# Two numbers loaded first on ScalarE's queue, and a narrower bias table, in an attention and feed-forward kernel

## The chip, the cores and the metric

The kernel runs on one core of a Trainium2 chip. The metric is device time in microseconds (us) of one execution; several executions are timed and their median is given. Engines are named as the profile names them: PE is TensorE's matmul and PEld its weight load, DVE is VectorE, ACT is ScalarE, POOL is GpSimd and SP is SyncE, which here only issues transfers.

## The reference: what is computed

An attention over 2 batches, 8 heads, 768 positions and head width 64 comes first. A query sees a key if the key is one of the first `n_global` (8) positions, or lies 0 to `n_local`-1 (95) positions behind it. Its score gets a bias that falls with the distance. Both numbers are inputs (int64), so the kernel must read them at run time.

```python
rel = pos[:, None] - pos[None, :]
is_global = pos[None, :] < int(n_global)
is_local = (rel >= 0) & (rel < int(n_local))
keep = is_global | is_local
dist = np.where(is_global & ~is_local, float(n_local), np.abs(rel))
bias = -slopes[:, None, None] * dist[None, :, :]
scores = np.where(keep, scores + bias, -1e9)
a = softmax(scores)          # over keys
x = a @ v                    # then rows of 512
g = elu(x @ w_in)            # 1536 x 2048
x = g @ w_out                # 1536 x 512
h = max(x @ w1, x @ w2, x @ w3)   # 1536 x 768
return h @ w_out2
```

## The kernel before, in words

**Stages.** The attention is cut into 96 steps: a step is one pair of heads (`hp`) and one tile of 128 queries (`t`) of a group of 256 rows (`g`). A query tile needs only the 96 keys before it, the 8 global keys and its own 128 keys: 232 columns (`WIN = PREV + G + P`), or 128 for the first tile of a batch. Each step goes over the engines in turn. PE makes the scores (`scores_pe`, L217), DVE adds the bias and takes the minimum (`scores_dve`, L243), ACT takes the exponential and its row sum (`scores_act`, L264), DVE adds 1e-9 to the sum, inverts it and scales (`sums` L226, `recip` L255, `norm` L277), PE transposes (`turn_pe`, L287 and L293), ACT copies the transpose to SBUF (`turn_act`, L304), and PE multiplies with the values (`values_pe`, L316). The first 18 steps run in `windowed`, one after the other with steps interleaved, and between them the first feed-forward weights are unpacked from 64-bit words to 32 bits (`c_rebase`, `c_low`, `c_word`, `c_high`, `c_rest`). The others run inside the feed-forward loop (`Feed.run`), where PE's matmuls of 128x512 take most of the time.

**The order of the work is written by hand** (`tc.manual_schedule()`): each engine does its instructions in the order of the program text, and each queue of transfers is issued in that order too. Before the first step, `windowed` does the following.

- SP loads the queries and keys of the first pair of steps (`load_pair(0)`, L179), then the two numbers into `ni` (L51, in `numbers`), then the queries and keys of the next two pairs.
- POOL clears a tile `z`, and PE multiplies it by itself 8 times (`warm`, L587 and L593), a filler. Two more such fillers on `ident` follow each of the first two steps' scores.
- POOL writes position tables (`positions`, L79): `rel`, the distance of each of 360 columns, and the key number, in a scratch tile `sc`. The 360 columns are four pieces: 128 for a first tile (`P`), 96 keys before (`PREV`), 8 global keys (`G`), and 128 own keys. Only the first and the third piece can hold a global key; the other two get a key number of 2^20. Then POOL writes the scale of each head (`qsc`, L103) and `ident`, and scales the queries of each pair as it lands (`scale_queries`, L187).
- DVE sends negative distances to 1e30 (L144, L145), turns the loaded numbers from int64 to floats (L53, L56, L60), and makes the bias table from them (`bases`). It does four passes over all 360 columns: L155 marks columns with `rel >= nl`, L156 marks keys that aren't global, L157 joins the first mark with `rel`, and L158 takes the smaller of that and of `max(key mark, nl)`.

DVE's first score step (L243) reads the finished `rel`, so it stands behind all of this.

Of the kernel before, what the change touches and what calls it, by code (L numbers as in the profile page):

```python
# [13 lines left out]
I32 = mybir.dt.int32  # L14
# [3 lines left out]
ALU = mybir.AluOpType  # L18
# [5 lines left out]
P = 128  # L24
# [5 lines left out]
G = 8  # L30
PREV = 96
EXT = P + G
WIN = PREV + G + P
CH = WIN // 2
BIG = 1e30
# [9 lines left out]

def numbers(nc, pool, n_ap):

    ni = pool.tile([P, 4], I32, name="ni")  # L50
    nc.sync.dma_start(ni, n_ap.bitcast(I32).partition_broadcast(P))  # L51
    w = pool.tile([P, 4], F32, name="nw")
    nc.vector.tensor_copy(w, ni)  # L53
    w2 = w.rearrange("p (a b) -> p a b", b=2)
    hi = pool.tile([P, 2], F32, name="nhi")
    nc.vector.scalar_tensor_tensor(  # L56
        hi, w2[:, :, 0], 0.0, w2[:, :, 1], op0=ALU.is_lt, op1=ALU.add
    )
    nf = pool.tile([P, 2], F32, name="nf")
    nc.vector.scalar_tensor_tensor(  # L60
        nf, hi, 4294967296.0, w2[:, :, 0], op0=ALU.mult, op1=ALU.add
    )
    return nf[:, 0:1], nf[:, 1:2]


def covered(nc, pool, ng, nl, flag):

    f = pool.tile([P, 4], F32, name="nok")
    nc.vector.tensor_scalar(f[:, 0:1], ng, 0.0, None, op0=ALU.is_ge)
    nc.vector.tensor_scalar(f[:, 1:2], ng, float(G), None, op0=ALU.is_le)  # L70
    nc.vector.tensor_scalar(f[:, 2:3], nl, 1.0, None, op0=ALU.is_ge)
    nc.vector.tensor_scalar(f[:, 3:4], nl, float(PREV + 1), None, op0=ALU.is_le)
    ok = pool.tile([P, 1], F32, name="ok")
    nc.vector.tensor_reduce(ok, f, axis=AX.X, op=ALU.min)
    nc.vector.tensor_copy(flag, ok)


def iota(nc, t, num, step, base, cm):
    nc.gpsimd.iota(  # L79
        t, [[step, num]], base=base, channel_multiplier=cm,  # L80
        allow_small_or_imprecise_dtypes=True,
    )
# [15 lines left out]
def query_scales(nc, pool):  # L98

    qsc = pool.tile([P, HP], F32, name="qsc")  # L100
    for hp in range(HP):
        for u in range(2):
            nc.gpsimd.memset(  # L103
                qsc[u * D:u * D + D, hp:hp + 1], -(2.0 ** (2 * hp + u + 1)) * D ** -0.5
            )
    return qsc


class Windowed:
# [17 lines left out]
    def positions(self, scratch):  # L127

        nc, c = self.nc, self.const
        n = P + WIN  # L130
        rel = c.tile([P, n], F32, name="rel")
        key, neg = scratch[0][:, 0:n], scratch[1][:, 0:n]
        far = 1 << 20
        o = 0
        for num, step, base, cm, kstep, kbase in (
            (P, -1, 0, 1, 1, 0),
            (PREV, -1, PREV, 1, 0, far),
            (G, 0, far, 0, 1, 0),
            (P, -1, 0, 1, 0, far),
        ):  # L140
            iota(nc, rel[:, o:o + num], num, step, base, cm)
            iota(nc, key[:, o:o + num], num, kstep, kbase, 0)
            o += num
        nc.vector.tensor_scalar(neg, rel, 0.0, BIG, op0=ALU.is_lt, op1=ALU.mult)  # L144
        nc.vector.tensor_tensor(rel, rel, neg, op=ALU.max)  # L145
        self.qsc = query_scales(nc, c)
        self.ident = c.tile([P, P], F32, name="ident")
        make_identity(nc, self.ident)
        self.base, self.key, self.tmp = rel, key, neg

    def bases(self, ng, nl, a, b):


        nc, rel, key, t = self.nc, self.base[:, a:b], self.key[:, a:b], self.tmp[:, a:b]
        nc.vector.tensor_scalar(t, rel, nl, BIG, op0=ALU.is_ge, op1=ALU.mult)  # L155
        nc.vector.tensor_scalar(key, key, ng, BIG, op0=ALU.is_ge, op1=ALU.mult)  # L156
        nc.vector.tensor_tensor(t, t, rel, op=ALU.max)  # L157
        nc.vector.scalar_tensor_tensor(rel, key, nl, t, op0=ALU.max, op1=ALU.min)  # L158

    def geom(self, s):  # L160

# [608 lines left out]
def dense_attention(tc, ctx, io, xd):  # L770
# [4 lines left out]
    p2 = ctx.enter_context(tc.tile_pool(name="dp", bufs=2))  # L775
    ps = ctx.enter_context(tc.tile_pool(name="dps", bufs=1, space=PSUM))
    ng, nl = numbers(nc, c, io["nn"])
    qsc = query_scales(nc, c)
    ident = c.tile([P, P], F32, name="ident")
# [69 lines left out]
def windowed(tc, ctx, io, flag):  # L849
    nc = tc.nc  # L850
    f = Feed(tc, ctx, io)
    at = Windowed(tc, ctx, io, f.ps, f.xy, f.wt, f.act)
    with tc.manual_schedule():
        scratch = [f.cv.tile([P, 512], F32, tag="wr", name="sc") for _ in range(2)]
        at.load_pair(0, True)
        f.warm(WARM)
        at.positions(scratch)
        ng, nl = numbers(nc, at.const, io["nn"])
        for p in range(1, 3):
            at.load_pair(p, True)  # L860
        at.scale_queries(0)
        at.bases(ng, nl, 0, P + WIN)
        first = BLOCKS[0] // GRP * 8
        x = f.split_tiles()

        def convert():
            f.c_rebase(0)
            f.c_low(0)
            yield
            f.c_word(0, 0)  # L870
            yield
            f.c_word(0, 1)
            yield
            f.c_high(0)
            f.c_rebase(1)
            f.c_low(1)
            yield
            f.c_word(1, 0)
            yield
            f.c_rest(0)  # L880
            yield
            f.c_word(1, 1)
            yield
            f.c_high(1)
            f.c_rebase(2)
            f.c_low(2)
            yield
            f.c_rest(1)
            yield
            f.c_word(2, 0)  # L890
            yield
            f.c_word(2, 1)
            yield

        words = convert()
        h = f.ps.tile([P, 512], F32, tag="h", name="h")
        for k in range(first + 2):
            e = k % 2
            at.load_values(k, True)
            if e == 0:  # L900
                at.load_pair(k // 2 + 3, k < first)
                at.scale_queries(k // 2 + 1)
            if k <= first:
                at.scores_pe(k, (("S0", "S1"), ("y0", "y1"))[e], 1 + (k == first))
            if k >= first:
                f.product(h, f.w[0][:, 0], x, GRP, 0, (k - first) * 6, 6)
            at.values_pe(k - 3)
            at.turn_pe(k - 2, ("TX", "y2", "y3")[k % 3])
            if k < FILL[0]:
                f.fill(at.ident, FILL[1])  # L910
            at.scores_dve(k, True)
            at.values_high(k - 3, x)
            at.turn_act(k - 2, nc.scalar.copy)
            at.scores_act(k)
            at.sums(k - 1)
            at.recip(k - 1)
            at.norm(k - 1)
            at.values_low(k - 3, x)
            if k >= CONV:
                next(words, None)  # L920
            if k in WLOAD:
                f.w_load()
        at.values_pe(first - 1)
        at.turn_pe(first, "TX")
        at.values_high(first - 1, x)
        at.turn_act(first, nc.scalar.copy)
        at.sums(first + 1)
        at.values_low(first - 1, x)
        at.recip(first + 1)
        at.norm(first + 1)  # L930
        next(words, None)
        f.run(at, first + 2, x, h, lambda: covered(nc, at.const, ng, nl, flag))
# [105 lines left out]
```

## Time and profile before

| | before |
|---|---|
| median of 3 runs | 570.06 us (569.61 to 570.16) |
| profiled execution, its own time | 570.73 us |
| span of the profiled execution | 568.7 us |
| mean granted TensorE clock, share of 2.4 GHz | 0.991 |
| PE busy, share of the span | 547.9 us, 96% |
| DVE busy | 323.9 us, 57% |
| ACT busy | 267.9 us, 47% |
| POOL busy | 77.8 us, 14% |

The span runs from the first to the last instruction of one execution; 2.0 us of that execution's own time lie around it. Busy shares are means over stages with different limits: DVE is nearly full in the first 150 us and idle for much of the rest, and PE is the other way about in the first 50 us.

### The profile page before, as it was taken

What the parts mean: (1) busy time and instruction counts of PE and PEld (TensorE: products, weight loads), DVE (VectorE), ACT (ScalarE), POOL (GpSimd) and SP (SyncE); (2) the same over time, 40 slices, a digit from 0 to 9 for tenths busy, and PEclk for the clock granted to TensorE, in tenths of its full rate; (3) what the DMA queues carried; (4) which work ended last, traced back from release to release, by engine and by line L of the source; (5) the groups of instructions that cost most, each with busy time, mean ns of one, the idle gap of its engine ahead of it and who ended that gap; (6) DMA issues with size and microseconds to landing.
All of it is one profiled execution on the core that took longest, in us unless ns stands there. A gap on an engine that the chain in (4) does not pass through costs nothing. (4 is left out here: it accounts for less than half of the span.)

```text
span 568.7 us, 7611 instructions
## 1 busy us (share of the span) xinstructions
PE 547.9 (96%) x2772; PEld 434.2 (76%) x2772; DVE 323.9 (57%) x732; ACT 267.9 (47%) x574; POOL 77.8 (14%) x87
## 2 busy tenths in 40 slices
PE   8788999999999999999999999999999999999995
PEld 6457777777777777777888888888887888888884
DVE  7998999999755444343466656567754112312112
ACT  5877777777656455554555564524323101311011
POOL 4100222222210000000011221023320000000000
PEclk9979999999999999999999999999999999999998
DMA  8918444432211111010013323122302000010002
GB/s 295 379 45 328 172 156 159 168 133 65 77 39 43 42 41 42 20 55 2 0 38 111 94 92 112 37 75 80 118 24 76 0 1 1 15 60 1 0 1 80
DMA packets 16670, 46.62 MB, mean 82 GB/s; under 512 B 1776, under 2 KB 1776, under 8 KB 16624
## 3 DMA queue, kind: packets, MB, share of 16 engines
q1 hardware_dynamic: 15760, 44.47, 22.9%
q10 hardware_dynamic: 864, 1.57, 0.8%
q8 instruction: 24, 0.39, 0.3%
q14 instruction: 22, 0.18, 0.1%
HBM read 42.90 MB, written 3.15 MB: 81 GB/s over the span
## 5 line engine op out<-in xcount | busy, mean ns | idle before, releaser
L505 PE MATMUL h<-xh,w 128*128 128x512 f32 (+1 forms) x536 | 144.3, 391 | 0.6 <-ACT xh L485 0.6
L505 PEld LDWEIGHTS h<-xh,w 128*128 128x128 f32 x536 | 98.3, 188 | 23.7 <-issue 1.7
L536 PE MATMUL y<-gh,w 128*128 128x512 f32 x384 | 98.7, 399 | 0.0
L512 ACT CAST gh<-e 128x512 fp32r<-128x512 f32 x66 | 41.1, 622 | 101.8 <-DVE e L725 87.1
L725 DVE TENSOR_TENSOR e<-S,e 128x512 f32<-128x512 f32 x36 | 24.9, 692 | 103.6 <-PE S L505 100.5
L536 PEld LDWEIGHTS y<-gh,w 128*128 128x128 f32 x384 | 69.6, 188 | 18.1 <-issue 1.5
L505 PE MATMUL h<-xl,w 128*128 128x512 f32 (+1 forms) x268 | 82.0, 387 | 0.0
L505 PE MATMUL S<-xh,w 128*128 128x512 f32 x288 | 77.0, 389 | 0.0
L530 DVE SCALAR_TENSOR_TENSOR e<-e,h 128x512 f32<-128x512 f32 x48 | 33.0, 687 | 68.0 <-ACT e L526 68.0
L505 PEld LDWEIGHTS S<-xh,w 128*128 128x128 f32 x288 | 54.1, 188 | 11.2
L525 ACT ACTIVATE e<-h 128x512 f32<-128x512 f32 x48 | 28.4, 592 | 67.7 <-PE h L505 67.4
L462 POOL TENSOR_TENSOR w<-wr,w 128x512 fp32r<-128x512 f32 x24 | 35.3, 1473 | 166.0 <-ACT w L461 166.0
L505 PEld LDWEIGHTS h<-xl,w 128*128 128x128 f32 x268 | 50.0, 188 | 10.5 <-DVE xl L486 0.2
L517 DVE TENSOR_TENSOR gl<-e,gh 128x512 fp32r<-128x512 f32 x50 | 39.8, 796 | 31.8 <-ACT gh L512 31.6
L264 ACT ACTIVATE p<-p,m 128x232 f32<-128x232 f32 (+1 forms) x96 | 44.8, 468 | 25.4 <-DVE m L243 25.4
L544 PE MATMUL y<-gl,w 128*128 128x512 f32 x192 | 51.5, 390 | 0.0
L415 DVE SCALAR_TENSOR_TENSOR wr<-wr 128x1024 uint32<-128x1024 uint32 (+1 forms) x36 | 50.0, 1397 | 0.7
L505 PE MATMUL S<-xl,w 128*128 128x512 f32 x144 | 44.3, 389 | 0.0
L451 DVE SCALAR_TENSOR_TENSOR wr<-wr 128x512 uint32<-128x512 uint32 x48 | 43.0, 896 | 2.2
L544 PEld LDWEIGHTS y<-gl,w 128*128 128x128 f32 x192 | 36.0, 188 | 7.9 <-issue 0.3
L569 PE MATMUL y<-w,gh 128*128 128x512 f32 x144 | 37.3, 390 | 0.4 <-POOLq L942 0.4
L517 POOL TENSOR_TENSOR gl<-e,gh 128x512 fp32r<-128x512 f32 x16 | 21.0, 1311 | 104.9 <-ACT gh L512 104.9
(85 smaller groups left out, 600.2 us busy)
## 6 DMA issues: line engine op xcount, KB each, us to landing
wr<-wa SPq DMA_DIRECT2D x14, 1024.0 KB, 7.6
wr<-wb SPq DMA_DIRECT2D x24, 512.0 KB, 3.3
v<-v SPq DMA_DIRECT2D x24, 256.0 KB, 2.7
raw<-qk SPq DMA_DIRECT2D x16, 312.0 KB, 3.3
raw<-qk SPq DMA_DIRECT2D x8, 260.0 KB, 3.4
wr<-wa SPq DMA_DIRECT2D x4, 512.0 KB, 3.7
out<-ot ACTq DMA_DIRECT2D x6, 256.0 KB, 3.0
out<-ot SPq DMA_DIRECT2D x6, 256.0 KB, 2.5
```

Of the source, the lines that this page charges most:

```text
L264: self.nc.scalar.activation(p[:, o], p[:, o], AF.Exp, bias=m[:, u:u + 1], scale=-1.0, accum_out=m[:, 2 + u:3 + u],)
L415: self.nc.vector.scalar_tensor_tensor(r[..., 0], r[..., 1], v, r[..., 0], op0=op, op1=ALU.bitwise_or)
L451: self.nc.vector.scalar_tensor_tensor(t, a, c, t, op0=op, op1=ALU.bitwise_or)
L462: nc.gpsimd.tensor_tensor(w[:, j % 2, 1], v, w[:, j % 2, 0].bitcast(F32), op=ALU.subtract)
L505: nc.tensor.matmul(out[:, o:n], w[:, part % 2, c * P:c * P + P], (xl if part == 2 else xh)[:, c, o:n], start=c == 0 and part == 0, stop=c ...
L512: self.nc.scalar.copy(gh[:, 0:n], e[:, 0:n])
L517: (engine or self.nc.vector).tensor_tensor(gl[:, 0:n], e[:, 0:n], gh[:, 0:n].bitcast(F32), op=ALU.subtract)
L525: self.nc.scalar.activation(e, h, AF.Relu, scale=-1.0)
L530: self.nc.vector.scalar_tensor_tensor(e, e, -1.0, h, op0=ALU.add, op1=ALU.max)
L536: self.nc.tensor.matmul(y[e][:, 0:n], w[:, a, e * P:e * P + P], g[0][:, 0:n], start=fc == 0 and a == 0, stop=False,)
L544: self.nc.tensor.matmul(y[e][:, 0:n], w[:, 0, e * P:e * P + P], g[1][:, 0:n], start=False, stop=fc == NFC - 1,)
L569: nc.tensor.matmul(o[r], gh[:, r * P:r * P + P], w[:, a], start=j == 0 and a == 0, stop=False,)
```

## The change

The load of the two numbers leaves `numbers` and becomes `load_numbers`. In `windowed` it is the first thing issued, and it goes on ACT's queue in place of SP's. The other half of `numbers` (the conversion) now stands behind the loads of pairs 1 and 2 in the text. `positions` writes key numbers only for the two pieces that can hold a global key, which drops two iotas. `bases` does two passes over 360 columns (mark, then join into `rel`), and two passes (key mark, then minimum) over the 128 and over the 8 columns where a key can be global. Line numbers behind L50 move by up to 10: `norm` is L286 after the change, `scores_dve` L252.

```diff
-def numbers(nc, pool, n_ap):
-
+def load_numbers(nc, pool, n_ap):
     ni = pool.tile([P, 4], I32, name="ni")
-    nc.sync.dma_start(ni, n_ap.bitcast(I32).partition_broadcast(P))
+    nc.scalar.dma_start(ni, n_ap.bitcast(I32).partition_broadcast(P))
+    return ni
+
+
+def numbers(nc, pool, n_ap, ni=None):
+
+    ni = load_numbers(nc, pool, n_ap) if ni is None else ni
     w = pool.tile([P, 4], F32, name="nw")
...
-        for num, step, base, cm, kstep, kbase in (
-            (P, -1, 0, 1, 1, 0),
-            (PREV, -1, PREV, 1, 0, far),
-            (G, 0, far, 0, 1, 0),
-            (P, -1, 0, 1, 0, far),
+        for num, step, base, cm, keys in (
+            (P, -1, 0, 1, True),
+            (PREV, -1, PREV, 1, False),
+            (G, 0, far, 0, True),
+            (P, -1, 0, 1, False),
         ):
             iota(nc, rel[:, o:o + num], num, step, base, cm)
-            iota(nc, key[:, o:o + num], num, kstep, kbase, 0)
+            if keys:
+                iota(nc, key[:, o:o + num], num, 1, 0, 0)
             o += num
...
-    def bases(self, ng, nl, a, b):
-
-
-        nc, rel, key, t = self.nc, self.base[:, a:b], self.key[:, a:b], self.tmp[:, a:b]
-        nc.vector.tensor_scalar(t, rel, nl, BIG, op0=ALU.is_ge, op1=ALU.mult)
-        nc.vector.tensor_scalar(key, key, ng, BIG, op0=ALU.is_ge, op1=ALU.mult)
-        nc.vector.tensor_tensor(t, t, rel, op=ALU.max)
-        nc.vector.scalar_tensor_tensor(rel, key, nl, t, op0=ALU.max, op1=ALU.min)
+    def bases(self, ng, nl):
+
+
+        v, rel, key, t = self.nc.vector, self.base, self.key, self.tmp
+        v.tensor_scalar(t, rel, nl, BIG, op0=ALU.is_ge, op1=ALU.mult)
+        v.tensor_tensor(rel, t, rel, op=ALU.max)
+        for o in (slice(0, P), slice(P + PREV, P + PREV + G)):
+            v.tensor_scalar(key[:, o], key[:, o], ng, BIG, op0=ALU.is_ge, op1=ALU.mult)
+            v.scalar_tensor_tensor(
+                rel[:, o], key[:, o], nl, rel[:, o], op0=ALU.max, op1=ALU.min
+            )
...
+        ni = load_numbers(nc, at.const, io["nn"])
         at.load_pair(0, True)
         f.warm(WARM)
         at.positions(scratch)
-        ng, nl = numbers(nc, at.const, io["nn"])
         for p in range(1, 3):
             at.load_pair(p, True)
+        ng, nl = numbers(nc, at.const, io["nn"], ni)
         at.scale_queries(0)
-        at.bases(ng, nl, 0, P + WIN)
+        at.bases(ng, nl)
```

DVE's order at the start, before the change, from the end of the position tables to the first score step (`nf` holds the two numbers as floats, `sc` is scratch, `S_153` and `S_154` are the scores of the first step's two heads):

```order
L53 CAST nw<-ni 128x4
L56 SCALAR_TENSOR_TENSOR nhi<-nw 128x2
L60 SCALAR_TENSOR_TENSOR nf<-nhi,nw 128x2
L155 TENSOR_SCALAR sc<-rel,nf 128x360
L156 TENSOR_SCALAR sc<-sc,nf 128x360
L157 TENSOR_TENSOR sc<-sc,rel 128x360
L158 SCALAR_TENSOR_TENSOR rel<-sc,nf 128x360
L243 ISA p,m<-S_153,rel 128x128
```

The same place after the change:

```order
L58 CAST nw<-ni 128x4
L61 SCALAR_TENSOR_TENSOR nhi<-nw 128x2
L65 SCALAR_TENSOR_TENSOR nf<-nhi,nw 128x2
L161 TENSOR_SCALAR sc<-rel,nf 128x360
L162 TENSOR_TENSOR rel<-sc,rel 128x360
L164 TENSOR_SCALAR sc<-sc,nf 128x128
L165 SCALAR_TENSOR_TENSOR rel<-sc,nf,rel 128x128
L164 TENSOR_SCALAR sc<-sc,nf 128x8
L165 SCALAR_TENSOR_TENSOR rel<-sc,nf,rel 128x8
L252 ISA p,m<-S_153,rel 128x128
```

Two passes of 360 columns have become two of 128 and two of 8, and `sc`'s pass no longer stands between the mark and the join.

ACT's order at the start, after the change (before, the load of the exponential's table was its first row, and the numbers' transfer was the second on SP):

```order
L50 DMA ni<-nn 128x4
L273 ACT_TABLE_LOAD
L273 ACTIVATE p,m<-p,m 128x128 x2
L273 ACTIVATE p,m<-p,m 128x232 x2
L313 COPY p<-y_192 128x256
```

The transfer stands ahead of the table load on ACT, and no transfer stands ahead of it on that queue.

POOL's position tables, after the change (before, an iota on `sc` followed each of the four on `rel`):

```order
L84 IOTA rel 128x128
L84 IOTA sc 128x128
L84 IOTA rel 128x96
L84 IOTA rel 128x8
L84 IOTA sc 128x8
L84 IOTA rel 128x128
L108 MEMSET qsc 64x1 x8
```

The 96-wide and the second 128-wide iota on `sc` are gone; on the other engines no row has moved.

## Rows read from the trace of the kernel before

**Rows 1.** Busy time by stretch; columns: stretch, length, PE, PEld, DVE, ACT, POOL, PEclk, DMA.

```profile
20.00:25.00 5.00, 3.24 (x28) 2.03 (x28) 4.86 (x18) 3.93 (x15) 0.40 (x1) 1.00 1.04 396
28.00:29.70 1.70, 0.32 (x5) 0.00 (x1) 1.63 (x11) 1.70 (x4) 0.00 (x0) 0.99 0.11 43
29.70:36.40 6.70, 6.70 (x36) 4.23 (x38) 6.56 (x22) 4.31 (x15) 0.00 (x0) 0.50 0.26 88
45.00:47.00 2.00, 0.66 (x8) 0.42 (x9) 1.93 (x9) 1.57 (x6) 0.00 (x0) 1.00 1.01 412
50.00:57.00 7.00, 6.94 (x48) 5.54 (x49) 5.49 (x13) 6.39 (x13) 1.29 (x1) 1.00 0.87 318
200.00:300.00 100.00, 99.99 (x522) 79.38 (x521) 45.15 (x121) 50.42 (x110) 3.59 (x4) 1.00 0.10 31
```

**Rows 2.** Timeline, DVE's start; columns: start us, us, instruction, count, [idle before <-releaser].

```profile
2.49 0.53 DVE L145 TENSOR_TENSOR rel<-rel,sc 128x360 f32<-128x360 f32 x1
4.02 0.20 DVE L53 CAST nw<-ni 128x4 f32<-128x4 int32 x1 [0.99 <-DMA ni<-nn]
...
4.54 0.16 DVE L60 SCALAR_TENSOR_TENSOR nf<-nhi,nw 128x2 f32<-128x2 f32 x1
4.74 0.41 DVE L155 TENSOR_SCALAR sc<-rel,nf 128x360 f32<-128x360 f32 x1
5.06 0.40 DVE L156 TENSOR_SCALAR sc<-sc,nf 128x360 f32<-128x360 f32 x1
5.38 0.53 DVE L157 TENSOR_TENSOR sc<-sc,rel 128x360 f32<-128x360 f32 x1
5.94 0.69 DVE L158 SCALAR_TENSOR_TENSOR rel<-sc,nf 128x360 f32<-128x360 f32 x1
6.78 0.29 DVE L243 CUSTOM_DVE_ANT_0 p<-S,rel 128x128 f32<-128x128 f32 x1 [0.16 <-DVE rel L158]
...
7.53 0.40 DVE L243 CUSTOM_DVE_ANT_0 p<-y,rel 128x232 f32<-128x232 f32 x1
```

**Rows 3.** Timeline, SP's queue, its first two issues.

```profile
0.73 0.40 SPq L179 DMA_DIRECT2D raw<-qk  x1
1.18 0.42 SPq L51 DMA_DIRECT2D ni<-nn  x1
```

**Rows 4.** Line L51, the numbers' transfer, from issue to landing.

```profile
DMA to landing us min/median/max: 2.8/2.8/2.8
```

**Rows 5.** Line L747, six output stores on ACT's queue, from issue to landing.

```profile
DMA to landing us min/median/max: 2.0/3.0/4.4
```

**Rows 6.** Timeline, ACT's first instruction.

```profile
0.73 1.28 ACT L264 ACT_TABLE_LOAD   x1 [0.73 <-PEq L1028]
```

**Rows 7.** Timeline, POOL: the dropped iotas, the first scaling.

```profile
1.50 0.21 POOL L79 IOTA sc<- 128x96 f32 x1
...
2.02 0.24 POOL L79 IOTA sc<- 128x128 f32 x1
...
4.02 0.48 POOL L187 TENSOR_SCALAR raw<-raw,qsc 128x256 f32<-128x256 f32 x1
```

**Rows 8.** Timeline, DVE: narrow passes, and scaling pairs with and without POOL beside them.

```profile
8.43 0.72 DVE L277 TENSOR_SCALAR p<-p,m 128x128 f32<-128x128 f32 x2
...
11.67 0.48 DVE L277 TENSOR_SCALAR p<-p,m 128x128 f32<-128x128 f32 x2
12.07 0.28 DVE L332 TENSOR_TENSOR xl<-y,xh 128x128 fp32r<-128x128 f32 x1
...
13.21 0.59 DVE L277 TENSOR_SCALAR p<-p,m 128x232 f32<-128x232 f32 x2
...
26.42 0.82 DVE L277 TENSOR_SCALAR p<-p,m 128x232 f32<-128x232 f32 x2
```

**Rows 9.** Timeline, PEld and PE: the scores of the first two steps.

```profile
4.70 0.51 PEld L217 LDWEIGHTS S<-raw 64*128 64x128 f32 x4 [0.22 <-POOL raw L187]
...
6.22 0.66 PE L217 MATMUL y<-raw 64*128 64x232 f32 x4
```

## Prediction
> **What bounds the kernel now.** I read the table of busy time by stretch first, because the page's share for PE (96%) is a mean over stages with different limits. From 20 to 25 us DVE is busy 4.86 of 5.00 us while PE has 3.24; from 200 to 300 us PE is busy 99.99 of 100.00 [rows 1]. So the opening is DVE's, the body PE's. The chain of waits that ended last is PE from start to end and tells nothing of the opening, so I turned to DVE's timeline there. DVE stands idle 0.99 us until the two numbers land, converts them, makes the bias table from 4.74 us on, and starts its first score step at 6.78, released by that table [rows 2]. From 6.78 on DVE hardly stops. Everything the change touches lies ahead of 6.78, on the chain load, conversion, table, first score. What that chain gains should pass through a saturated DVE into a saturated PE and to the end, unless another engine or a transfer takes its place.
>
> **The load.** SP issues it second, at 1.18 us, behind the first pair's queries at 0.73 [rows 3], and it lands 2.8 us later [rows 4], just ahead of its reader at 4.02. Now ACT issues it as its first instruction; ACT, whose table load starts at 0.73 today [rows 6], is ready at the same time as SP. With the same 2.8 us the numbers come 1.18 - 0.73 = 0.45 us earlier, and the conversion starts at 3.57. Bounds come from the nearest transfers on ACT's queue, six output stores that took 2.0 to 4.4 us [rows 5]. At 2.0 us the reader would be held by the pass L145 instead, which ends at 2.49 + 0.53 = 3.02 us and moves 0.17 us with POOL's iotas (one dropped iota stands ahead of `rel`'s last): 2.89, a gain of 1.1. At 4.4 us the numbers land at 5.13, a loss of 1.15. I take 2.8, since that is this very transfer. The table load behind it on ACT starts about 0.4 us later and ends near 2.4 us; ACT's first exponential waits for the score step at 6.78, so this costs nothing.
>
> **The table.** Today it takes 6.78 - 4.74 = 2.04 us from its first pass to the score step [rows 2]. The new six passes, start to start: the mark of 360 columns, 0.41 and 0.04 of hand-over (from L60's end, 4.54 + 0.16 = 4.70, to 4.74), 0.45; the join, 0.53 long, with a successor that doesn't read its result and so may start 0.09 earlier, as L156 does behind L155 (0.32 against 0.41), 0.44; the key mark of 128 columns, 0.28 (the pair takes 0.48 and its second starts 0.20 later [rows 8]) and hand-over, 0.32; the minimum of 128 columns, priced as the 128-wide tensor pass of 0.28 less 0.09, 0.20; two passes of 8 columns at 0.20 each, as L60 to L155. The sum is 1.81, a gain of 0.23, say 0.25. Bounds: with every pass paying its whole length and hand-over it is 0.45 + 0.57 + 0.32 + 0.32 + 0.20 + 0.20 = 2.06, no gain; with the last three overlapped and no hand-over about 1.55, a gain of 0.5.
>
> A rule speaks against this edit. The Trainium skill, VectorE: DVE Perf Modes, section "The TRN2 errata — SBUF-src ops pay a fixed extra latency per instruction", puts a measured fixed term of about 150 cycles (0.156 us) on each instruction beside its columns; four passes would then cost 4 x 0.156 + 1080/960 = 1.75 us and six 6 x 0.156 + 744/960 = 1.71 (estimates, with plain scalar passes at two columns a cycle), a gain of 0.04. L145 agrees with the fixed term ((360 + 151)/960 = 0.53 us), but L156's start 0.32 us behind a pass of 0.41 shows that part of it overlaps.
>
> **POOL, SP and PE.** The two dropped iotas are each followed 0.17 to 0.18 us later by the next instruction, so POOL's first scaling, at 4.02 now [rows 7], comes 0.35 us earlier, at 3.67; the first pair lands at 0.73 + 2.8 = 3.53 and doesn't hold it. PE's first scores waited 0.22 us for that scaling [rows 9], so PE moves up by up to 0.22. SP's later issues move up by 0.45 us; no consumer in the opening waits on those loads except POOL, which has time. Nothing else is moved: the fallback path also loses and gains rows, but isn't run.
>
> **Sum.** 0.45 + 0.25 = 0.70 us: the first score step at about 6.08. PE caps it: the second step's scores end at 6.22 + 0.66 = 6.88, less 0.22 is 6.66, and DVE reads the last of them at 7.53 now, 6.83 then. So the cap is just clear; a faster landing would gain 0.87 at most. The cover for the shift afterwards is DVE's own load. Against the profiled execution's 570.73 us that makes 570.0; that execution stands 0.67 above the median of the runs, so I subtract from the median: 570.06 - 0.70 = **569.4 us**.
>
> **Rivals.**
> 1. *The gain halves or goes*: six passes pay in full (table gain 0), or ACT's queue lands at its stores' 3.0 us or later (load gain 0.25 or less). By the first alone 570.06 - 0.45 = 569.6; by both 569.8. For it: L157 to L158 takes 0.56, no overlap, where one reads the other. Against it: L155 to L156.
> 2. *Collisions with POOL vanish*: three of DVE's scaling pairs, the first at 8.43 and the last at 26.42, take 0.24 us more than the same pair elsewhere (0.72 against 0.48, 0.82 against 0.59 [rows 8]); each falls beside one of POOL's scalings, whose times follow the landings. DVE moves by 0.70 and the landings by 0.3 to 0.45, so some may part: 3 x 0.24 = 0.72 more, 568.6. Against it: others may meet instead.
> 3. *The clock drops in a costly place* (slower). PE's granted clock goes to 0.50 (1.2 GHz) from 29.7 to 36.4 us, behind a stretch in which PE was busy 0.32 of 1.70; it costs nothing, since DVE is full there (6.56 of 6.70). From 45 to 47 PE is as idle (0.66 of 2.00) and no drop follows. From 50 to 57 PE has 6.94 of 7.00 [rows 1]. If the shift let such a drop begin by 50, half of 6.7 us, 3.35, would be lost: 570.06 - 0.70 + 3.35 = 572.7. It decides from the moment the drop covers PE's full stretch. Against it: the runs before, within 0.55 us, show no sign of it.
> 4. *The load isn't first*: the table load holds it, issue at 0.73 + 1.28 = 2.01, landing at 4.81, 0.83 late, less 0.25: 570.6. Against it: the order of ACT's rows.
>
> **How the numbers follow.** Forecast 0.57, rival 1 0.18, rival 2 0.13, rival 3 0.07, rival 4 0.05. A measurement here can tell about 0.2%, 1.14 us: under 568.92 is faster, over 571.20 slower. Faster comes from rival 2 and a little of the forecast's upper end, 0.16; slower from rival 3 and the worst landing, 0.09; within, 0.75. The range takes in rivals 1, 2 and 4 and leaves out rival 3: 568.6 to 570.6.
>
> **What would show it.** The numbers' issue on ACT at 0.73 and a reader near 3.6; table passes spaced 0.45, 0.44, 0.32, 0.20, 0.20, 0.20; the first score near 6.1 in place of 6.78; the same lead, 0.6 to 0.8 us, at the first matmul of 512 columns near 51 us and at the end. I am wrong if the reader is no earlier than 4.0, if the lead is lost before 50 us, or if the granted clock is low in another stretch.

## The result, and the profile after

The change makes the kernel slower, by 0.7%. Over 20 runs each the median goes from 569.73 us to 575.05 us; the ratio of after to before is 1.0066 with a 95% interval of 1.0042 to 1.0089. The times lie in two groups, and the change moves runs from one to the other: before, 17 of 20 runs stand at 568.7 to 570.9 us and 3 at 575.3 to 575.7; after, one stands at 570.2 and 19 at 573.3 to 576.6. The median so jumps by a whole group; the means of the 20 times, 570.58 and 574.94, lie 4.4 us apart. The profiled execution after took 575.05 us with a span of 573.0 us and a mean granted clock of 0.978, against 568.7 us and 0.991 before.

**The loads.** The timelines of ACT's and SP's queues after the change, with the first issue of each:

```profile
0.74 0.41 ACTq L50 DMA_DIRECT2D ni<-nn  x1
```

```profile
0.73 1.35 SPq L188 DMA_DIRECT2D raw<-qk  x3
```

The numbers' issue moved as planned, from 1.18 [rows 3] to 0.74. Issue to landing of that load (its line's view) and of the first three loads of queries and keys:

```profile
DMA to landing us min/median/max: 4.3/4.3/4.3
```

```profile
DMA to landing us min/median/max: 4.1/4.4/4.6
```

The numbers now take 4.3 us in place of 2.8 [rows 4]. The first pair, the quickest of the three, takes 4.1 us in place of 2.8; before the change it had landed by about 3.5 us, ahead of its reader, POOL's first scaling, at 4.02 [rows 7].

**DVE's start after**, its timeline to the first score step:

```profile
2.33 0.53 DVE L151 TENSOR_TENSOR rel<-rel,sc 128x360 f32<-128x360 f32 x1
5.02 0.40 DVE L58 CAST nw<-ni 128x4 f32<-128x4 int32 x1 [2.15 <-DMA ni<-nn]
...
5.84 0.52 DVE L161 TENSOR_SCALAR sc<-rel,nf 128x360 f32<-128x360 f32 x1
6.40 0.54 DVE L162 TENSOR_TENSOR rel<-sc,rel 128x360 f32<-128x360 f32 x1
6.86 0.42 DVE L164 TENSOR_SCALAR sc<-sc,nf 128x128 f32<-128x128 f32 x1
7.32 0.35 DVE L165 SCALAR_TENSOR_TENSOR rel<-sc,nf,rel 128x128 f32<-128x128 f32 x1
7.59 0.23 DVE L164 TENSOR_SCALAR sc<-sc,nf 128x8 f32<-128x8 f32 x1
7.85 0.35 DVE L165 SCALAR_TENSOR_TENSOR rel<-sc,nf,rel 128x8 f32<-128x8 f32 x1
8.12 0.28 DVE L252 CUSTOM_DVE_ANT_0 p<-S,rel 128x128 f32<-128x128 f32 x1
```

The wait for the numbers grew from 0.99 to 2.15 us, the conversion starts at 5.02 instead of 4.02, and the table takes 8.12 - 5.84 = 2.28 us instead of 2.04 [rows 2]. The first score step is 1.34 us late.

**PE's start after**, its timeline, and POOL's first two scalings:

```profile
0.98 3.79 PE L602 MATMUL z<-z 128*128 128x128 f32 x16 [0.98 <-POOL z L596]
5.45 0.49 PE L226 MATMUL S<-raw 64*128 64x128 f32 x4 [0.68 <-POOL raw L196]
...
8.51 0.65 PE L226 MATMUL S<-raw 64*128 64x128 f32 x4 [0.70 <-POOL raw L196]
10.30 0.52 PE L296 MATMUL y<-ident,p 128*128 128x128 f32 x2 [1.14 <-DVE p L286]
...
20.05 1.15 PE L226 MATMUL y<-raw 64*128 64x232 f32 x4
```

```profile
4.91 0.48 POOL L196 TENSOR_SCALAR raw<-raw,qsc 128x256 f32<-128x256 f32 x1 [1.29 <-DMA raw<-qk]
5.69 0.48 POOL L196 TENSOR_SCALAR raw<-raw,qsc 128x256 f32<-128x256 f32 x1 [0.29 <-DMA raw<-qk]
```

The first scaling waits 1.29 us for the first pair, and PE, whose fillers are done, waits for that scaling (0.68 us), then 0.70 us until 8.51, and, before the first transpose, for the late scaling in `norm` on DVE (1.14 us). Such waits of PE are called holes below. The profile puts the second down to POOL, but the second pair's scaling had ended by 6.17. The third step's scores go into the tiles that DVE reads in its first score step, and here and in experiments 1, 2, 3, 7, 8 and 9 they start 0.38 to 0.40 us behind the start of that step (8.12 here). So the first hole comes with the late first pair and the second with the late numbers. Before, the first was 0.22 us of weight load [rows 9], the second wasn't there, and the third was nearly as long (1.08 us).

**What follows**, busy time by stretch after the change (columns as in [rows 1]):

```profile
10.00:15.00 5.00, 4.70 (x30) 2.83 (x30) 4.46 (x27) 3.36 (x14) 0.48 (x1) 0.70 1.03 401
15.00:20.00 5.00, 5.00 (x26) 2.91 (x26) 3.14 (x19) 3.21 (x12) 0.76 (x2) 0.50 1.04 394
20.00:25.00 5.00, 5.00 (x26) 2.81 (x26) 3.88 (x19) 3.51 (x12) 0.80 (x2) 0.50 0.48 173
25.00:30.00 5.00, 5.00 (x27) 2.78 (x28) 4.88 (x15) 3.78 (x14) 1.10 (x1) 0.59 0.75 239
...
200.00:300.00 100.00, 99.99 (x532) 79.18 (x533) 44.78 (x126) 50.42 (x113) 2.76 (x4) 1.00 0.10 32
```

The granted clock falls to 0.50 (1.2 GHz) near 12 us and stays there until about 29; the same four score matmuls take 1.15 us in place of 0.66 [rows 9]. And here DVE isn't full: from 20 to 25 us it has 3.88, where it had 4.86 [rows 1]. Its timeline there says on whom it waits:

```profile
18.47 0.29 DVE L252 CUSTOM_DVE_ANT_0 p<-S,rel 128x128 f32<-128x128 f32 x1 [0.67 <-PE S L226]
...
21.23 0.40 DVE L252 CUSTOM_DVE_ANT_0 p<-y,rel 128x232 f32<-128x232 f32 x1 [0.58 <-PE y L226]
...
23.97 0.40 DVE L252 CUSTOM_DVE_ANT_0 p<-S,rel 128x232 f32<-128x232 f32 x1 [0.41 <-PE S L226]
```

By the first matmul of 512 columns the kernel is 4.90 us behind; PE's timelines before and after:

```profile
52.02 1.65 PE L505 MATMUL h<-xh,w 128*128 128x512 f32 x6
```

```profile
56.92 1.65 PE L514 MATMUL h<-xh,w 128*128 128x512 f32 x6
```

If the late head passes on whole, it is 1.34 us of that and the low clock the other 3.6 us; experiment 11 divides it otherwise. Later stages gain 0.6 us back, and the span ends 4.3 us later.

### The profile page after: what moved, and what is told of

It is laid out like the page before. It is cut to its first block, busy times and chain, and to the rows that moved or that the text cites. A ratio compares the mean times of both kernels' runs of the same rounds, so it can differ in the third digit from the quotient of the medians.

```text
span 573.0 us, 7613 instructions
## 1 busy us (share of the span) xinstructions
PE 554.3 (97%) x2772; PEld 437.9 (76%) x2772; DVE 324.2 (57%) x734; ACT 268.5 (47%) x574; POOL 78.0 (14%) x85
```

## The experiments

Each was timed against the kernel before on the same chip. "Above 573" counts runs above 573 us; those of the kernel before, in the three comparisons, were 3 of 29 (experiments 1 to 4), 6 of 32 (5 to 8; one run that took three times as long is left out) and 3 of 29 (9 to 12).

**Experiment 1: the numbers second on SP again.** The changed kernel; experiments 4 and 7 have the same new argument of `load_numbers`.

```diff
-def load_numbers(nc, pool, n_ap):
+def load_numbers(nc, pool, n_ap, queue=None):
     ni = pool.tile([P, 4], I32, name="ni")
-    nc.scalar.dma_start(ni, n_ap.bitcast(I32).partition_broadcast(P))
+    (queue or nc.scalar).dma_start(ni, n_ap.bitcast(I32).partition_broadcast(P))
...
-        ni = load_numbers(nc, at.const, io["nn"])
         at.load_pair(0, True)
+        ni = load_numbers(nc, at.const, io["nn"], nc.sync)
```

> The changed kernel with the numbers' load put back on SP's queue, second; table and iotas stay narrow. Queue theory (the load on ACT's queue beside three loads back to back on SP's lands late, 4.3 us after issue, delays the first pair's queries from 2.8 to 4.1 us, and the holes this leaves on PE bring the low clock from 12 to 28 us): numbers land 2.8 us after issue, first score step near 6.5, the low clock begins near 29 us again, time 569.0 to 570.0. Table theory (six dependent passes instead of four, 2.28 us against 2.04, shift the program into the low clock): still 573 or more.

Median 570.62 us, ratio 1.0034 (1.0008 to 1.0061), 3 of 12 above 573. The numbers took 2.8 us, the first pair 2.9, and the clock fell between 25 and 30 us, as expected. The first score step came at 6.76, against 6.78 before and the 6.5 expected: the new table took 2.14 us. The median is 0.6 us above the range expected, but far from the table theory's 573. So the queue is the larger part of the loss, and the table gains nothing.

**Experiment 2: only the load moved.** The kernel before with the load split from `numbers`, first on ACT's queue.

```diff
...
-    nc.sync.dma_start(ni, n_ap.bitcast(I32).partition_broadcast(P))
+    nc.scalar.dma_start(ni, n_ap.bitcast(I32).partition_broadcast(P))
...
+        ni = load_numbers(nc, at.const, io["nn"])
         at.load_pair(0, True)
         f.warm(WARM)
         at.positions(scratch)
-        ng, nl = numbers(nc, at.const, io["nn"])
+        ng, nl = numbers(nc, at.const, io["nn"], ni)
```

> The kernel before with the numbers' load first on ACT's queue, and nothing else; table and iotas as before. Queue theory: the numbers land 4 us or more after issue, first score step near 7.9, low clock from about 12 us, time 573 to 576. Table theory: 569.0 to 570.5.

Median 575.59 us, ratio 1.0078 (1.0041 to 1.0114), 7 of 9 above 573; numbers 4.3 us, first pair 4.2, first score step 8.11. The load alone makes the whole loss.

**Experiment 3: the changed kernel again.**

> The changed kernel once more, for a second trace and its spread. Queue theory: first score step 7.5 to 8.5 in every trace, time about 575. Chance theory (a mode of the chip that has nothing to do with the change): a trace with the first score step near 6 to 7 and a time near 570 is as likely as one near 575.

Median 574.78 us, ratio 1.0074 (1.0045 to 1.0103), 6 of 9 above 573. A second trace shows the same: numbers 4.3 us, first pair 4.2, a hole of 1.04 us on PE before the first scores, clock low from 10.8 us.

**Experiment 4: the numbers first on SP.**

```diff
...
-        ni = load_numbers(nc, at.const, io["nn"])
+        ni = load_numbers(nc, at.const, io["nn"], nc.sync)
         at.load_pair(0, True)
```

> The changed kernel with the numbers' load first on SP's queue, ahead of the first pair's queries. Queue theory: nothing runs beside it, so it lands 2.0 to 2.8 us after issue at 0.73; the first pair's queries come 0.45 us later than before, near 4.0; first score step 5.9 to 6.3, time 568.8 to 569.8. Table theory: 573 or more.

Missed: median 572.67 us, ratio 1.0037 (0.9993 to 1.0080), 6 of 12 above 573. In the trace, of the longest of the 12 runs (577.58 us), the numbers took 3.4 us, though nothing was ahead of them, and the first pair 4.0 from its issue at 1.18, so PE had a hole of 1.40 us and the first score step came at 7.15. The other six runs lie at 568.7 to 570.1; no trace shows what differed in them.

**Experiment 5: the change with a longer warm-up on PE.**

```diff
-WARM = 8
+WARM = 11
```

> The changed kernel with 11 in place of 8 fillers on PE ahead of the first scores (two passes each, about 0.43 us a filler), so that they last to about 5.8 us and the hole of 1.0 us before the first scores is gone; the numbers still land near 5.0. Hole theory (the early low clock follows PE's hole while it waits for the first pair's queries, and is worth some 4 us of the loss): most runs leave the group at 574 to 577 and stand at 570.0 to 571.5, 1.0 to 1.3 above the kernel before for the late table. Rival (the late table alone, through DVE, costs all of it): still 574 or more.

Median 574.02 us, ratio 1.0060 (1.0030 to 1.0090), 7 of 12 above 573: missed, as the median stands where the rival put it. But the trace, of a run of 571.61 us, shows no low clock before 30 us although the first score step is at 8.21, so a late table doesn't bring the low clock in every run. The first two holes were gone, while one of 1.14 us before the first transpose was left (from 9.25 to 10.38 us). Experiment 11 narrows that one too.

**Experiment 6: the hole alone, in the kernel before.**

```diff
-WARM = 8
+WARM = 6
```

> The kernel before with 6 in place of 8 fillers: PE's fill ends near 3.6 us, a hole of about 1.1 us before the first scores, while the numbers, the table and all loads stay as before. Hole theory: most runs go to 574 to 576 though nothing on DVE is late. Rival (late table): 569.7, as before.

Median 575.53 us, ratio 1.0064 (1.0031 to 1.0097), 11 of 12 above 573. PE's timeline and one stretch:

```profile
0.98 2.93 PE L593 MATMUL z<-z 128*128 128x128 f32 x12 [0.98 <-POOL z L587]
4.57 0.80 PE L217 MATMUL S<-raw 64*128 64x128 f32 x4 [0.66 <-POOL raw L187]
5.30 1.22 PE L593 MATMUL z<-ident 128*128 128x128 f32 x4
6.45 1.15 PE L217 MATMUL y<-raw 64*128 64x232 f32 x4
```

```profile
15.00:20.00 5.00, 5.00 (x28) 3.02 (x26) 3.14 (x19) 3.12 (x12) 0.48 (x1) 1.00 1.03 385
```

The table isn't late here: the first score step is at 6.80. Yet from 5.3 us on the matmuls take the times they take at 1.2 GHz (1.15 us for four), from 15 to 20 us DVE has 3.14 of 5.00, as after the change, and the first matmul of 512 columns starts at 57.44, 5.42 us later than before. So less filler, with the hole of 0.66 us that it leaves, costs the time of the upper group by itself. It isn't quite the same event: here PE's matmuls are slow from the first scores on and stay so until about 31 us, while after the change four of 64x128 took 0.49 us, the short time, at 5.45 us, and the clock fell later, near 12 us.

**Experiment 7: the numbers third on SP.**

```diff
...
-        ni = load_numbers(nc, at.const, io["nn"])
         at.load_pair(0, True)
+        at.load_pair(1, True)
+        ni = load_numbers(nc, at.const, io["nn"], nc.sync)
```

> The changed kernel with the numbers third on SP's queue, behind the second pair's queries, so that the first two big loads are issued back to back and nothing is on ACT's queue. Spacing theory (the first pair lands late because the second pair's load follows it 0.45 us sooner): the first pair lands 4.0 us or more after issue, as with the change. ACT-queue theory (it is late because a transfer on the other queue runs beside it): 2.8 to 2.9 us. Either way the numbers land near 5 us or later, and the time is 572 or more unless PE has no hole.

The first pair took 2.8 us, the second, issued right behind it, 3.0: the spacing theory falls. The third pair, now behind the numbers, took 4.3. Median 574.31 us, ratio 1.0060 (1.0024 to 1.0096), 7 of 10 above 573; the numbers landed at 4.9 and PE had holes of 0.62 and 0.94 us. The first pair was on time, so the first hole is missing; the late numbers and the 0.62 us that come with them are enough to put most runs above 573. The trace is of one of the three runs below 573 (570.58 us).

**Experiment 8: the change with a spacer.**

```diff
         at.load_pair(0, True)
+        spare = at.const.tile([P, 4], I32, name="spare")
+        nc.sync.dma_start(spare, io["nn"].bitcast(I32).partition_broadcast(P))
```

> The changed kernel with a second load of the same two numbers, into a tile that nobody reads, on SP between the first and the second pair's queries. Spacing theory: the first pair lands 2.8 to 3.0 us after issue again, the numbers on ACT's queue by 3.5 to 3.7 us, first score step near 6.2, time 568.8 to 569.8. ACT-queue theory: the first pair still lands 4.0 us or more after issue and the time stays at 573 to 576.

Between the two: the first pair took 3.6 us, the numbers 3.7, the second pair 5.2, behind two small loads. Median 570.84 us, ratio 1.0020 (0.9981 to 1.0059), 4 of 12 above 573.

**Experiment 9: only a spare load on ACT's queue, in the kernel before.**

```diff
+        spare = at.const.tile([P, 4], I32, name="spare")
+        nc.scalar.dma_start(spare, io["nn"].bitcast(I32).partition_broadcast(P))
         at.load_pair(0, True)
```

> The kernel before, and as ACT's first instruction a second load of the two numbers into a tile that nobody reads; all else, the numbers' own load second on SP included, stays. Theory (the small load beside the big ones is what makes them land late): the first pair lands 3.6 to 4.2 us after issue in place of 2.8, PE has a hole of 0.5 us or more before the first scores, the numbers land at 4.5 to 6 us, most runs at 573 to 577. Rival (the late landing comes from SP's missing second issue): the first pair stays at 2.8 us and the time at 569.7.

Median 576.14 us of 4 runs, all above 573, ratio 1.011 (1.006 to 1.016). From the timelines of POOL, DVE and PE:

```profile
4.35 0.48 POOL L187 TENSOR_SCALAR raw<-raw,qsc 128x256 f32<-128x256 f32 x1 [0.30 <-DMA raw<-qk]
```

```profile
6.10 0.17 DVE L53 CAST nw<-ni 128x4 f32<-128x4 int32 x1 [3.07 <-DMA ni<-nn]
```

```profile
0.98 3.78 PE L593 MATMUL z<-z 128*128 128x128 f32 x16 [0.98 <-POOL z L587]
4.89 0.80 PE L217 MATMUL S<-raw 64*128 64x128 f32 x4
...
6.77 1.15 PE L217 MATMUL y<-raw 64*128 64x232 f32 x4
```

A load that nobody reads makes the first pair take 3.5 us instead of 2.8 and the numbers 4.9 instead of 2.8. The small load itself delays what runs beside or behind it. The transfer engines weren't full meanwhile; busy time from 4 to 5 us (columns as in [rows 1], then GB/s):

```profile
4.00:5.00 1.00, 0.87 (x6) 0.58 (x5) 0.00 (x0) 0.00 (x0) 0.54 (x2) 1.00 0.03 1
```

The 16 DMA engines are busy 0.03 of that time, while the numbers and the next two pairs are issued and haven't landed.

One part of the expectation missed: the hole before the first scores is 0.13 us (from 4.76 to 4.89), not 0.5 or more, and still PE's matmuls are slow from there on, as in experiment 6. So a hole isn't the only way into the low clock; what kept it low here stays open.

**Experiments 10 to 12: PE's second hole filled.** In 10 the numbers are second on SP (experiment 1), in 11 it is the change with the longer warm-up (experiment 5), in 12 the kernel before; each with

```diff
-FILL = 2, 2
+FILL = 2, 5
...
-            if k < FILL[0]:
-                f.fill(at.ident, FILL[1])
+            if k < 2:
+                f.fill(at.ident, FILL[k])
```

> The changed kernel with the numbers second on SP, and 5 in place of 2 fillers behind the second step's scores, so that PE's hole of about 1 us before the first transpose shrinks to a few tenths. Hole theory: the runs at 574 to 577 (3 of 12 without the fillers) go, all 12 lie between 568.5 and 571, median 569.3. Rival (those runs are chance): 2 to 4 of 12 remain.

> The changed kernel with both fills, 11 fillers at the start and 5 behind the second step's scores. Hole theory: with hardly a hole left before 11 us the slow group (7 of 12 with the first fill alone) shrinks to 2 of 12 or fewer, and the rest stands 1.0 to 1.5 above the kernel before, 570.3 to 571.6. Rival (the late table costs it): 574 or more.

> The kernel before with 5 in place of 2 fillers behind the second step's scores, and nothing else. Hole theory: its own slow runs (8 of 32 in the last comparison) go, 0 or 1 of 12 above 573, median 569.3 to 569.8. Rival (chance): 2 to 4 of 12 remain.

(The 8 of 32 there count two runs at 572.3 and 572.9.)

| | median us | ratio | above 573 |
|---|---|---|---|
| 10 | 569.46 | 0.9982 (0.9953 to 1.0011) | 1 of 12 |
| 11 | 570.38 | 1.0014 (0.9989 to 1.0039) | 1 of 12 |
| 12 | 569.56 | 0.9990 (0.9969 to 1.0011) | 0 of 11 |

The hole before the first transpose shrank to 0.46, 0.87 and 0.59 us in their traces. In experiment 11 the first score step, PE's score matmuls near 20 us and the first matmul of 512 columns stand here:

```profile
8.14 0.28 DVE L252 CUSTOM_DVE_ANT_0 p<-S,rel 128x128 f32<-128x128 f32 x1
```

```profile
20.56 0.66 PE L226 MATMUL y<-raw 64*128 64x232 f32 x4
...
52.73 1.65 PE L514 MATMUL h<-xh,w 128*128 128x512 f32 x6
```

Its head is as late as after the change (8.14 against 8.12 us), but the four score matmuls take 0.66 us, not 1.15, and the feed-forward begins 4.19 us sooner (52.73 against 56.92): that is the low clock's price. The late head, 1.36 us at the first score step, is 0.71 us at that matmul (52.73 against 52.02 before) and 570.38 - 569.58 (the kernel before in that comparison) = 0.8 us in the medians, which the interval doesn't tell from nothing. That the fills and not chance took the runs down is clear in 11: 1 of 12 above 573, against 7 of 12 with the first fill alone and 25 of 29 for the changed kernel (19 of 20 and 6 of 9). 10 and 12 can't be told from each other or from the median of the kernel before, and whether they have fewer runs above 573 isn't shown: 0 of 11 against 3 of 29 can be chance.

## Why the prediction was wrong

It forecast 569.4 us; 575.05 was measured. Two prices failed, both of the moved load: what it takes itself, and what it costs the load beside it. Each opened a hole on PE, which the prediction's sum doesn't have, and the low clock that followed is the larger part of the loss (about 4.2 us by experiment 11). Two of the signs that I had named came: the reader at 5.02 us, not before 4.0, and a low clock in another stretch, from 12 to 29 us.

- **The load: the first step that failed.** "I take 2.8, since that is this very transfer." It took 4.3 us, near the end that I had kept as a bound (4.4), and came 1.0 us later instead of 0.45 earlier. The 2.8 us was the price of a transfer second on SP's queue, not of one beside it on ACT's; first on SP it took 3.4 (experiment 4). Earlier issue bought nothing. The Trainium skill, DMA: Bandwidth & Descriptors, section "Issuing engines are not separate DMA queues", says that transfers from all issuing engines run on the same 16 DMA engines and interleave. Experiment 9 agrees in that a load on ACT's queue delays SP's loads (from 2.8 us to 3.5 for the first pair and 4.9 for the numbers); with the engines busy 0.03 from 4 to 5 us there, it doesn't show that sharing them is the cause.
- **"The first pair lands at 0.73 + 2.8 = 3.53 and doesn't hold it": the second step that failed.** It landed at about 4.8 us. I priced what the moved load would cost itself and nothing for what it does to its neighbours. This opened the first of PE's holes (0.68 us). The second (0.70 us) came with the late numbers, and experiment 7, which has it without the first, has 7 of 10 runs above 573.
- **The table.** Predicted 1.81 us, a gain of 0.25; measured 1.97 to 2.36 in nine traces with the new table, and 1.95 to 2.27 in five with the old one: no gain, as my bound without overlap (2.06) had it. How long it takes varies with what POOL does beside it: the 128-column key mark took 0.42 us after the change, beside one of POOL's scalings, and 0.28 in experiment 1, clear of them. The Trainium skill, VectorE: DVE Perf Modes, section "The TRN2 errata — SBUF-src ops pay a fixed extra latency per instruction", has the fixed cost for each instruction from which the prediction estimated a gain of 0.04. That was nearer than my overlaps.
- **The first rival**, that the load's gain goes, was right in direction, and ended too early, at no gain.
- **The clock rival** had the right sign and about the right size (3.35 us against 4.2), but the wrong place and cause: I looked for a drop at 50 us from the shift, and took the one at 30 us as proof that a drop in the opening costs nothing, "since DVE is full there". That may hold at 30 us, where the steps carry weight conversions on DVE and it has 6.56 of 6.70 us; no run tests it. After the change the first conversion pass starts at 22.87 us, and before it, at half the clock, PE is the slower. PE has a hole of 1.08 us ahead of the first transpose in the kernel before too, and 15 of its own 110 runs lie above 573. That would fit if PE stood near the edge there, but no trace of such a run was kept.
- **Right**: ACT's table load cost nothing, POOL's iotas went (its first scaling was free at 3.6 us), and some of what is lost ahead of 10 us reaches the feed-forward: 0.71 us of a late head of 1.36 in experiment 11's trace, not the whole that the prediction's sum took.

What stays open: why a load of 2 KB, 16 bytes to each of 128 partitions, holds up loads of 260 KB by 0.7 to 1.5 us, and why after the change the first pair lost 1.3 us where experiment 9 lost 0.7. The next large load was issued right behind the first pair in the one and behind a second small load in the other, and without a load on ACT's queue that spacing cost nothing (2.8 us in experiment 7). The Trainium skill, DMA: Bandwidth & Descriptors, section "Specifications", says that below 512 B the engines read, modify and write. No run here tells that cause from another.

## What to carry to other kernels

Before a small load is given a queue of its own to come sooner, look at what lands beside it: here it came later and took the first big load with it. Filler work that keeps PE's clock up is timed against the loads it waits for; when a load moves, count the hole again. Whether a low clock costs time is read stage by stage: here it did where DVE had room (3.14 of 5.00 us).

## What the runs showed of the hardware

The small load delays by place: a 260 KB load took 2.7 to 2.9 us when issued ahead of it on the same queue, 3.0 right behind another big one (experiment 7), 3.8 to 4.4 right behind it on the same queue, and 3.5 to 4.2 beside it on the other. And the granted clock in the records isn't the whole story: in experiment 6 it reads 1.00 from 15 to 20 us, while the four matmuls take 1.15 us, as they do where it reads 0.50. The Trainium skill, TensorE: Matmul & The Clock Gate, section "Part 1: The HAM clock gate (the "warmup" mystery)", warns that such records can be unreliable. The durations of one instruction told it here.
